# Other costs, handovers and priorities for the list that orders an attention stage

## The chip, the cores and the metric

The kernel runs on one core of a Trainium2 chip. The metric is the device time of one execution in microseconds, the median of several. The core has TensorE (PE, with weight loads shown apart as PEld), VectorE (DVE), ScalarE (ACT) and GpSimd (POOL), each with a queue that it works through in order, and SyncE (SP), which only issues transfers here. Five queues run side by side and wait for one another by semaphores; what stands where in each queue is fixed when the program is built.

## The reference

Two parts follow each other: a recurrent attention and an MLP.

```python
# r, k, v, w, a, b: (4, 8, 768, 40); w in 0.85 to 0.95
for t in range(S):
    y[:, :, t] = np.einsum('bhd,bhde->bhe', rt, state)
    Sa = np.einsum('bhde,bhe->bhd', state, at)
    state_decay = state * wt[:, :, None, :] - np.einsum('bhd,bhe->bhde', Sa, bt)
    state = state_decay + np.einsum('bhd,bhe->bhde', vt, kt)
...
x = y.transpose(0, 2, 1, 3).reshape(3072, 320)
h = x @ w_in                                   # 320 x 2048
sp = np.where(h > 20.0, h, np.log1p(np.exp(np.minimum(h, 20.0))))
out = (h * np.tanh(sp)) @ w_out                # 2048 x 320
```

Each of the 32 pairs of batch and head has a 40x40 state that every one of the 768 time steps decays and updates.

## The kernel before

The 768 steps are cut into 12 chunks of 64. Within a chunk the recurrence becomes matrix products with a triangular matrix that has to be inverted; between chunks only the state passes. There are four kinds of work:

- **Preparation** (`pre_a`, lines 241 to 332), once for each chunk and each `be` of 2, so 24 times. SP loads wa (decay and a) and bk (b and k). DVE forms running products of the decay with two scans (L266, L271), scales a and bk by them (L269, L277) and takes reciprocals; ACT lays a out (L275); PE forms the products of a and bk (L306), which ACT and DVE move from PSUM into GP and HA (L309 to L317), and transposes bk into bkn (L329, L331). POOL stores the running decay (L280). There is one wa buffer and one bk buffer for each `be`; the next load waits for the last reader, for bk that is L329.
- **Inverse** (`inv`, lines 334 to 396), once for a pair of chunks, so 6 times. DVE transposes GP into X (L338), then runs 30 rounds of a product (L343) and a sum (L346), each needing the one before, then transposes X to TT (L348) and TT back (L350). Small 32x32 products on PE (L361, L369) complete the blocks, ACT assembles them in bdT (L383 to L385), and PE and ACT make the KT tiles of both chunks (L393, L396).
- **Step** (`step`, lines 401 to 534), once for a chunk, 12 in a row, each half g of the heads by itself: copy of the state (L419), product with KT (L429, L432), products with bdr (L469, L472), transposes (L442, L457), output and state products (L497, L502) and the state update on DVE (L482, L507, L513). POOL loads VS, UVT and bdr (L403, L407, L410) and stores the output y (L533).
- **Weight conversions** for the MLP (`Mlp.plan`, lines 631 to 653): float64 weights are loaded by SP as integer pairs, turned into float32 by bit operations on DVE (L645 to L649) and split into a high and a low part (L651, L652). A first block of them becomes possible when all preparations are done, a second when all inverses are done.

Buffers bound how far one kind may run ahead: two GP tiles (one a pair), eight HA and eight bkn tiles (four chunks), four KT tiles (two chunks), one X and one TT, four PSUM banks for preparation and inverse and four for the steps.

The order of all this is not written by hand. `Plan.op` collects the operations with an engine, a cost, a latency `lat` until others may use the result, and the tiles read and written, from which it derives who must come after whom. Claims on pool buffers (`Buf`) are not among these links. `Plan.order` then plays the list through: `tail` of an operation is the longest sum of costs and latencies from it to the end; the engine that can start something first is picked, and of its operations that can start within `look` = 0.05 us of the earliest, the one with the longest tail is taken. An operation that needs a pool buffer can't start before one is free. PE pays 0.13 for a change of tile mode. The result, sorted by start, is emitted, so that it fixes every queue. `late=LATE`, 15.0, stands on one operation only, the state update L513, once per chunk and half; through the chain of states it adds 15 to the tail for every chunk still to come.

The MLP (`Mlp.run`, lines 718 to 793) follows outside this list, in plain program order; its first matmul is L751.

Of the kernel before, what the change touches and what calls it, by code (L numbers as in the profile page):

```python
# [7 lines left out]
F32 = mybir.dt.float32  # L8
# [10 lines left out]
LATE = 15.0  # L19
# [10 lines left out]

class Plan:


    def __init__(self, look=0.05):
        self.ops, self.wr, self.rd, self.free, self.look = [], {}, {}, {}, look
# [7 lines left out]
    def op(self, eng, cost, fn, r=(), w=(), lat=0.15, mode=None, late=0.0, claim=()):  # L43
        o = Op()
        o.eng, o.cost, o.fn, o.lat, o.mode, o.late, o.i = eng, cost, fn, lat, mode, late, len(self.ops)
# [25 lines left out]
    def after(self, ops, fn):  # L71
        key = ('after', len(self.ops))
        o = self.op('0', 0.0, fn, w=[key], lat=0.0)
        for p in ops:
            if p.i not in o.pre:
                o.pre[p.i] = p
                p.post.append(o)
        return key

    def order(self):  # L80
        for o in reversed(self.ops):
            o.tail = o.cost + o.lat + max((p.tail for p in o.post), default=0.0) + o.late
            o.need = len(o.pre)
            o.ready = 0.0
        ready = [o for o in self.ops if not o.need]
        clock, mode, out = {}, {}, []
        while ready:
            best = None
            start = {}
            for o in ready:  # L90
                t = max(o.ready, clock.get(o.eng, 0.0))
                for b in o.bufs:
                    if b.t is None:
                        free = self.free[b.pool[0]]
                        t = max(t, min((f for f in free if f is not None), default=1e9))
                start[o] = t
# [4 lines left out]
            best = max((o for o in ready if o.eng == e and start[o] <= low[e] + self.look), key=lambda o: (o.tail, -o.i))  # L101
# [8 lines left out]
            c = best.cost  # L110
            if best.mode and mode.get(e) not in (None, best.mode):
                c += 0.13
            mode[e] = best.mode or mode.get(e)
            end = t + c
            clock[e] = end
            best.start = t
            out.append(best)
            ready.remove(best)
            for b in best.bufs:
                b.users -= 1  # L120
                b.end = max(b.end, end + best.lat)
# [52 lines left out]
def attention(ctx, tc, I, yD, pD, nch, M):  # L174
# [66 lines left out]
    def pre_a(c, be):  # L241
        wa, bk, ad = wab[be], bkb[be], adb[be]
        xo, og, ok, oa, oh = (0, 0, 64, 0, 40) if be == 0 else (0, 64, 0, 64, 0)
        for al in range(2):
            q = slice(al * 64, al * 64 + 40)
            op('S', 0.1, lambda q=q, al=al: SP.dma_start(out=wa[q], in_=I['wa'][c, be, al]), w=[('wz', be, al), ('a', be, al)], lat=2.5)
        for al in range(2):
            q = slice(al * 64, al * 64 + 40)
            op('S', 0.1, lambda q=q, al=al: SP.dma_start(out=bk[q, :, xo:xo + 128], in_=I['bk'][c, be, al]), w=[('bk', be, al)], lat=2.5)
        if (c, be) == (0, 0):  # L250
            op('S', 0.1, lambda: SP.dma_start(out=cst, in_=I['cst']), w=['cst'], lat=2.5)
# [12 lines left out]
        op('V', 0.35, lambda: V.tensor_reduce(out=w2.t[:, 0], in_=wz3[:, :, 1:33], axis=AX.X, op=ALU.mult), r=WZ, w=[w2])  # L264
        op('V', 0.14, lambda: V.reciprocal(d1[:, 64:584:65], w2.t[:, 0]), r=[w2], w=['d1'])
        op('V', 1.15, lambda: V.tensor_tensor_scan(out=P.t, data0=wz[:, 0:520], data1=d1[:, 64:584], initial=0.0, op0=ALU.mult,  # L266
                                                   op1=ALU.add), r=WZ + ['d1'], w=[P])
        op('V', 0.1, lambda: V.tensor_copy(w2.t[:, 1], P.t[:, 64:520:65]), r=[P], w=[w2])
        op('V', 0.62, lambda: V.tensor_tensor(out=a3, in0=a3, in1=p3()[:, :, 0:64], op=ALU.mult), r=[P], w=AA)  # L269
        op('V', 0.14, lambda: V.reciprocal(d1[:, 64:584:65], w2.t[:, 1]), r=[w2], w=['d1'])  # L270
        op('V', 1.15, lambda: V.tensor_tensor_scan(out=E[:, 0:519][:, ::-1], data0=wz[:, 2:521][:, ::-1], data1=d1[:, 1:520][:, ::-1],  # L271
                                                   initial=0.0, op0=ALU.mult, op1=ALU.add), r=WZ + ['d1'], w=['E'])
        for al in range(2):
            q = slice(al * 64, al * 64 + 64)
            op('A', 0.58, lambda q=q, al=al: A.copy(ad[q, :, :, al], a[q].rearrange("p (s k t) -> p s k t", k=2, t=32)),  # L275
               r=[('a', be, al)], w=[('ad', be, al)])
        op('V', 1.14, lambda: V.tensor_tensor(out=bk4, in0=bk4, in1=E3[:, :, 0:64].unsqueeze(2).broadcast_to([128, 8, 2, 64]),  # L277
                                              op=ALU.mult), r=['E'], w=BK)
        for al in range(2):
            op('G', 0.6, lambda al=al: G.dma_start(out=pD[c, be, :, al], in_=P.t[al * 64:al * 64 + 40]), r=[P], lat=1.5)  # L280
        if be == 1:
# [9 lines left out]
            op('P', 0.3, mm, r=ws + ['cst'], w=[b], mode=64, claim=[rw])  # L291
# [7 lines left out]
        for s0 in (0, 3, 6):  # L299
# [8 lines left out]
            op('P', 0.29 * m, mm, r=[('ad', be, 0), ('ad', be, 1), ('id', be)] + BK, w=[b], mode=128, claim=[gp, ha])  # L308
            op('A', 0.2, lambda s0=s0, m=m, pv=pv: A.mul(gp.t[0:64, u0 + s0:u0 + s0 + m, 1], pv()[0:64, 0:m, og:og + 32], -1.0),  # L309
               r=[b], w=[(gp, u0 + s0)])  # L310
            op('A', 0.27, lambda s0=s0, m=m, pv=pv: A.mul(gp.t[64:128, u0 + s0:u0 + s0 + m].rearrange("p u k i -> p u (k i)"),
                                                          pv()[64:128, 0:m, og:og + 64], -1.0), r=[b], w=[(gp, u0 + s0, 1)])
            op('A', 0.21, lambda s0=s0, m=m, pv=pv: A.copy(ha.t[:, s0:s0 + m, oa:oa + 40], pv()[:, 0:m, 128:168]), r=[b], w=[(ha, s0)])  # L313
            op('V', 0.27, lambda s0=s0, m=m, pv=pv: V.tensor_tensor(out=ha.t[:, s0:s0 + m, oh:oh + 64], in0=pv()[:, 0:m, ok:ok + 64],
                                                                    in1=maskH.unsqueeze(1).broadcast_to([128, m, 64]), op=ALU.mult),
               r=[b, 'cst'], w=[(ha, s0 + 1)])
        op('V', 0.36, lambda: V.tensor_tensor(out=gp.t[:, u0:u0 + 8, 1], in0=gp.t[:, u0:u0 + 8, 1],  # L317
# [5 lines left out]
        for s0 in (0, 4):  # L323
# [6 lines left out]
            op('P', 0.45, tr, r=BK + ['cst'], w=[b], mode=128, claim=[bkn])  # L330
            op('A', 0.38, lambda s0=s0, pv=pv: A.copy(bkn.t[:, s0 * 80:s0 * 80 + 320].rearrange("p (s a e) -> p s a e", a=2, e=40),  # L331
                                                     pv()[:, :, :, 0:40]), r=[b], w=[(bkn, s0)])

    def inv(n):
# [3 lines left out]
        op('V', 2.0, lambda: V.transpose(X.rearrange("p t j -> p j t"), gp.t[:, :, 1].rearrange("p u j -> p j u")), r=allg, w=['X'])  # L338
        op('V', 0.08, lambda: V.memset(X.rearrange("p t j -> p (t j)")[:, 0:1024:33], 1.0), w=['X'])
        for i in range(1, 31):  # L340
            m = 31 - i
            tv = tmp[:, 0:m * i].rearrange("p (t j) -> p t j", j=i)
            op('V', 0.16 + m * i * 0.001, lambda tv=tv, i=i, m=m: V.tensor_tensor(  # L343
                out=tv, in0=X[:, i + 1:32, i:i + 1].broadcast_to([128, m, i]), in1=X[:, i:i + 1, 0:i].broadcast_to([128, m, i]), op=ALU.mult),
               r=['X'], w=['tmp'], lat=0.0)
            op('V', 0.16 + m * i * 0.001, lambda tv=tv, i=i: V.tensor_tensor(out=X[:, i + 1:32, 0:i], in0=X[:, i + 1:32, 0:i], in1=tv, op=ALU.add),  # L346
               r=['tmp'], w=['X'], lat=0.0)
        op('V', 1.9, lambda: V.transpose(TT.rearrange("p u t -> p t u"), X), r=['X'], w=['TT'])  # L348
        T1 = lambda: gp.t[0:64, :, 0]
        op('V', 1.15, lambda: V.transpose(T1(), TT[0:64]), r=['TT'], w=[(gp, 'T1')])  # L350
        for h in range(2):
# [18 lines left out]
            op('P', 0.85, mx, r=['TT'] + gk(h), w=[bx], mode=32)  # L370
            op('A', 0.54, lambda xv=xv: A.copy(X2, xv()), r=[bx], w=['X2'])
            op('P', 0.85, my, r=[(gp, 'T1'), 'X2'], w=[by], mode=32)
            c = 2 * n + h
            
            for be in range(2):
# [4 lines left out]
                for al in range(2):  # L380
                    q0 = slice(al * 32, al * 32 + 32)
                    q1 = slice(64 + al * 32, 96 + al * 32)
                    op('A', 0.37, lambda bd=bd, q0=q0, us=us, al=al: A.copy(bd[q0, :, al, 0:32], TT[q0, us]), r=['TT'], w=[bdk[al * 3]])  # L383
                    op('A', 0.37, lambda bd=bd, q1=q1, us=us, al=al: A.copy(bd[q1, :, al, 32:64], TT[q1, us]), r=['TT'], w=[bdk[al * 3 + 1]])
                    op('A', 0.34, lambda bd=bd, q0=q0, al=al, yv=yv, be=be: A.copy(bd[q0, :, al, 32:64], yv()[q0, be * 8:be * 8 + 8]), r=[by],  # L385
                       w=[bdk[al * 3 + 2]])
                for s0 in (0, 4):
# [7 lines left out]
                    op('P', 0.9, mk, r=[(ha, k) for k in (0, 1, 3, 4, 6, 7)] + bdk, w=[b], mode=128, claim=[kt])  # L395
                    op('A', 0.54, lambda s0=s0, kv=kv, kt=kt: A.copy(kt.t[:, s0:s0 + 4], kv()), r=[b], w=[(kt, s0 // 4)])  # L396
# [18 lines left out]
    def step_a(c, g):  # L415
        st = ST[g]
        if c > 0:
            for be in range(2):
                op('A', 0.42, lambda be=be: A.copy(VS[be][srow[be], g, 0:320].rearrange("p (s d) -> p s d", d=40), st[srow[be], :, 0:40]),  # L419
# [11 lines left out]
        op('P', 1.0, mm, r=[(k, g) for k in kts] + [(x, be, g) for x in ('VSv', 'VSs') for be in range(2)], w=[b], mode=64)  # L431
        op('A', 0.56, lambda: A.mul(UVT.rearrange("p s (x t) -> p x s t", t=64)[:, 0:4:3, g * 4:g * 4 + 4], uv(), -1.0), r=[b], w=[('u', g)])  # L432

    def step_u(c, g):
        if c < nch - 1:
            for be in range(2):
# [6 lines left out]
                op('P', 0.45, tr, r=UV(g) + ['cst'], w=[b], mode=128)  # L443
                op('A', 0.38, lambda be=be, tv=tv: A.copy(UVQ[be][:, g * 8:g * 8 + 8, 64:104], tv()[:, :, :, 0:40].rearrange("p s a d -> p (s a) d")),
# [381 lines left out]
```

## Time and profile before

| | us |
|---|---|
| median of 3 runs | 893.96 (891.82 to 895.59) |
| the profiled execution's own time | 897.87 |
| its span, first to last instruction | 895.7 |
| first matmul of the MLP in it | 536.66 |
| PE busy / DVE busy / ACT busy | 733.2 / 477.8 / 425.5 |
| mean granted TensorE clock | 0.886 |

The profile shows one execution. Its page gives the busy time of each engine, the span in 40 equal slices with the busy share of each in tenths and the granted clock of TensorE (PEclk), the DMA queues, and the chain of work that ended last. Beside it there are views with the busy time by stretches of the span, with every instruction of one engine in order of time (start, duration, engine, line, operation, what it writes and reads, and in brackets the idle time before it with what ended it), and with the sums of all waits. A line number is that of the kernel before.

### The profile page before, as it was taken

Reading aid. Unit: us, or ns where it says so; the run is one execution under the profiler, and the core shown is the slowest. Engines: PE = TensorE matmul, PEld = TensorE weight load, DVE = VectorE, ACT = ScalarE, POOL = GpSimd, SP = SyncE. Lnnn points to the kernel's source line nnn. Section 1 sums busy time; section 2 is a strip of 40 time slices with the busy share of each in tenths; the row PEclk is TensorE's granted clock in tenths of the full one; section 3 lists DMA queues with packets and bytes.
Section 4 is the critical chain, followed back from the end, with each engine's and each line's share of the span. In section 5 each row is a group of like instructions: output and inputs, shape, how many; then the busy total and the mean of one; then the engine's idle time right before and its main releaser. Section 6 shows DMA issues by size and latency. Waiting matters only on the chain.

```text
span 895.7 us, 18823 instructions
## 1 busy us (share of the span) xinstructions
PE 733.2 (82%) x7816; PEld 705.3 (79%) x7816; DVE 477.8 (53%) x975; ACT 425.5 (48%) x937; POOL 101.5 (11%) x166
## 2 busy tenths in 40 slices
PE   2625885969597677959795939999999999999998
PEld 2515784968586676849684939999999999999998
DVE  5798488658946974895386579422222221222110
ACT  4423853665476455636554847433333333333331
POOL 7100211211220211112111200000000000000000
PEclk9655987789698969888896979999999999999999
DMA  7321522242223313222222376311111111110000
GB/s 166 95 52 31 129 67 69 77 105 68 68 65 92 90 37 86 74 75 59 61 78 78 108 244 166 84 36 52 33 33 37 51 33 34 36 33 16 15 1 30
DMA packets 58212, 61.91 MB, mean 69 GB/s; under 512 B 25536, under 2 KB 48704, under 8 KB 58128
## 3 DMA queue, kind: packets, MB, share of 16 engines
q1 hardware_dynamic: 49296, 40.94, 16.3%
q0 software_dynamic: 8832, 19.79, 8.8%
q8 instruction: 61, 1.00, 0.5%
q14 instruction: 23, 0.19, 0.1%
HBM read 48.79 MB, written 11.86 MB: 68 GB/s over the span
## 4 chain that ended last, share of the span: by engine, by line
PE 66%; DVE 17%; DMA 6%; ACT 6%; issue 3%; POOL 1%; SPq 1%; DVEq 0%; ACTq 0%; POOLq 0%
PE ph L751 21%; PE pr L306 7%; PE po L772 6%; PE po L773 6%; PE po L771 6%; DVE XL L346 5%; DVE tmp L343 5%; DMA bk<-in_bk 4%; PE pl L469 3%; PE pr L393 3%; PE pl L497 3%; PE pl L442 3%; PE pr L361 2%; PE pr L369 2%; DMA wa<-in_wa 2%
## 5 line engine op out<-in xcount | busy, mean ns | idle before, releaser
L751 PE MATMUL ph<-xh,w_ih 128*128 128x256 f32 x576 | 149.5, 285 | 14.7 <-ACT xh L734 14.7
L753 ACT ACTIVATE g<-ph 128x512 f32<-128x512 f32 x96 | 57.0, 597 | 187.8 <-PE ph L751 187.8
L757 DVE TENSOR_TENSOR gl<-g,gh 128x1024 fp32r<-128x1024 f32 x48 | 58.8, 1225 | 163.2 <-ACT gh L756 162.9
L306 PE MATMUL pr<-bk,ad 128*128 128x168 f32 x384 | 97.3, 418 | 52.9 <-ACT HA L313 17.8
L306 PEld LDWEIGHTS pr<-bk,ad 128*128 128x128 f32 x384 | 82.2, 266 | 60.5 <-ACT HA L313 20.2
L751 PE MATMUL ph<-xh,w_il 128*128 128x256 f32 x576 | 124.1, 284 | 0.0
L751 PEld LDWEIGHTS ph<-xh,w_ih 128*128 128x128 f32 x576 | 110.5, 192 | 15.1 <-ACT xh L734 15.0
L772 PE MATMUL po<-w_ol,gh 128*128 128x320 f32 x384 | 118.6, 309 | 0.0
L773 PE MATMUL po<-w_oh,gl 128*128 128x320 f32 x384 | 118.5, 309 | 0.0
L771 PE MATMUL po<-w_oh,gh 128*128 128x320 f32 x384 | 118.4, 308 | 0.0
L751 PE MATMUL ph<-xl,w_ih 128*128 128x256 f32 x384 | 101.3, 285 | 0.0
L751 PEld LDWEIGHTS ph<-xh,w_il 128*128 128x128 f32 x576 | 96.9, 192 | 0.0
L751 PEld LDWEIGHTS ph<-xl,w_ih 128*128 128x128 f32 x384 | 73.8, 192 | 0.1
L361 PE MATMUL pr<-TT,GP 32*32 32x32 f32 x768 | 21.7, 236 | 61.7 <-DVE TT L348 53.2
L771 PEld LDWEIGHTS po<-w_oh,gh 128*128 128x128 f32 x384 | 72.2, 188 | 0.0
L773 PEld LDWEIGHTS po<-w_oh,gl 128*128 128x128 f32 x384 | 72.1, 188 | 0.0
L772 PEld LDWEIGHTS po<-w_ol,gh 128*128 128x128 f32 x384 | 72.1, 188 | 0.0
L361 PEld LDWEIGHTS pr<-TT,GP 32*32 32x32 f32 x768 | 21.0, 151 | 63.0 <-DVE TT L348 34.8
L346 DVE TENSOR_TENSOR XL<-XL,tmp 128x30 f32<-128x30 f32 (+9 forms) x180 | 59.6, 331 | 5.6
L343 DVE TENSOR_TENSOR tmp<-XL 128x30 f32<-128x30 f32 (+9 forms) x180 | 59.6, 331 | 5.5
L393 PE MATMUL pr<-bdT,HA 128*104 128x128 f32 x384 | 54.8, 309 | 2.7 <-ACT HA L313 1.0
L393 PEld LDWEIGHTS pr<-bdT,HA 128*104 128x104 f32 x384 | 52.8, 201 | 4.6 <-ACT KT L396 1.6
(95 smaller groups left out, 1246.3 us busy)
## 6 DMA issues: line engine op xcount, KB each, us to landing
wa<-in_wa SPq DMA_DIRECT2D x48, 162.5 KB
bk<-in_bk SPq DMA_DIRECT2D x48, 160.0 KB
cv_d<-in_wi SPq DMA_DIRECT2D x12, 512.0 KB
cv_d<-in_wo SPq DMA_DIRECT2D x8, 640.0 KB
pD<-P POOLq DMA_DIRECT2D x48, 81.2 KB, 2.3
VS<-in_vN POOLq DMA_DIRECT2D x24, 160.0 KB, 3.0
bdr<-in_rD POOLq DMA_DIRECT2D x24, 160.0 KB, 4.5
UVT<-in_vD POOLq DMA_DIRECT2D x24, 160.0 KB, 3.7
```

What stands on the lines that cost most here:

```text
L306: PE.matmul(pv()[:, j], ad[:, s0 + j].rearrange("p k a t -> p (k a t)"), bk[:, s0 + j], start=(j == 0), stop=True, skip_group_check=True)
L343: op('V', 0.16 + m * i * 0.001, lambda tv=tv, i=i, m=m: V.tensor_tensor(out=tv, in0=X[:, i + 1:32, i:i + 1].broadcast_to([128, m, i]), in1 ...
L346: op('V', 0.16 + m * i * 0.001, lambda tv=tv, i=i: V.tensor_tensor(out=X[:, i + 1:32, 0:i], in0=X[:, i + 1:32, 0:i], in1=tv, op=ALU.add), ...
L361: PE.matmul(xv()[al * 32:al * 32 + 32, j], gp.t[q, u, 0], TT[q, u], start=(j == 0), stop=True, skip_group_check=True)
L393: PE.matmul(kv()[:, j], ha.t[:, s0 + j], bd[:, o + s0 + j].rearrange("p a t -> p (a t)"), start=(j == 0), stop=True, skip_group_check=True)
L442: PE.transpose(tv()[:, s].rearrange("p a d -> p (a d)"), UVT[:, g * 4 + s, be * 128:be * 128 + 128], ident)
L751: PE.matmul(o, w, x, start=(j == 0 and n == 0), stop=(n == 7), skip_group_check=True)
L753: A.activation(g[:, f0:f0 + 2], ph, AF.Mish)
L757: V.tensor_tensor(out=gl, in0=g, in1=gh.bitcast(F32), op=ALU.subtract)
L771: PE.matmul(po[k], gh[:, j, t], oh, start=(f == 0), stop=False, skip_group_check=True)
L772: PE.matmul(po[k], gh[:, j, t], ol, start=False, stop=False, skip_group_check=True)
L773: PE.matmul(po[k], gl[:, j, t], oh, start=False, stop=(f == 15), skip_group_check=True)
```

## The change

Only the arithmetic of the list and its numbers change; the operations, their tiles and the pool sizes stay. Every cost is replaced by a duration. An engine is taken to be free again after `occ`, 0.085 us before the end on DVE and 0.01 after it on ACT; a result is there after `fin`, which adds 0.16 on PE and, for transfers, a landing time; a dependent operation is ready `sem` later, 0.035 to 0.06 by its engine; a freed buffer costs 0.05. On PE the list keeps an account of busy time in windows of 4096/1200 = 3.41 us and from it a clock of 1.0 or 0.5; at 0.5 an operation takes `work` longer. LATE becomes 0.

```diff
-LATE = 15.0
+LOOK = 0.05
+LATE = 0.0
...
-    def op(self, eng, cost, fn, r=(), w=(), lat=0.15, mode=None, late=0.0, claim=()):
+    def op(self, eng, dur, fn, r=(), w=(), lat=None, mode=None, work=0.0, late=0.0, claim=(), tag=''):
...
+        o.occ = max(0.0, dur + dict(V=-0.085, A=0.01).get(eng, 0.0))
+        o.fin = dur + (lat if lat is not None else 0.16 if eng == 'P' else 0.0)
...
     def order(self):
+        sem = dict(V=0.035, A=0.035, P=0.053, S=0.06, G=0.06)
         for o in reversed(self.ops):
-            o.tail = o.cost + o.lat + max((p.tail for p in o.post), default=0.0) + o.late
+            o.tail = o.fin + 0.04 + max((p.tail for p in o.post), default=0.0) + o.late
...
+            occ, fin = best.occ, best.fin
+            if e == 'P':
+                if mode not in (None, best.mode):
+                    t += 0.095
+                mode = best.mode
+                while win < int(t / WINDOW):
+                    a = act.get(win, 0.0) / WINDOW
+                    clk = (1.0 if a >= 0.35 else 0.5) if clk == 1.0 else (1.0 if a >= 0.69 else 0.5)
+                    win += 1
+                if clk < 1.0:
+                    occ, fin = occ + best.work, fin + best.work + 0.04
...
+            clock[e] = t + occ
...
-                    self.free[b.pool[0]][b.k] = b.end
+                    self.free[b.pool[0]][b.k] = b.end + 0.05
...
-                p.ready = max(p.ready, end + best.lat)
+                p.ready = max(p.ready, t + fin + sem.get(p.eng, 0.0))
```

The numbers of the operations, some of about forty (the last number of a transfer is its landing):

```diff
-            op('S', 0.1, lambda q=q, al=al: SP.dma_start(out=wa[q], ...), ..., lat=2.5)
+            op('S', 0.45, lambda q=q, al=al: SP.dma_start(out=wa[q], ...), ..., lat=3.6)
-            op('S', 0.1, lambda q=q, al=al: SP.dma_start(out=bk[q, :, xo:xo + 128], ...), ..., lat=2.5)
+            op('S', 0.85, lambda q=q, al=al: SP.dma_start(out=bk[q, :, xo:xo + 128], ...), ..., lat=3.7)
-        op('V', 1.15, lambda: V.tensor_tensor_scan(out=P.t, ...
+        op('V', 1.235, lambda: V.tensor_tensor_scan(out=P.t, ...
-        op('V', 1.14, lambda: V.tensor_tensor(out=bk4, ...
+        op('V', 1.22, lambda: V.tensor_tensor(out=bk4, ...
-            op('P', 0.29 * m, mm, ..., mode=128, claim=[gp, ha])
+            op('P', 0.286 * m, mm, ..., mode=128, work=0.28 * m, claim=[gp, ha])
-            op('V', 0.16 + m * i * 0.001, ..., r=['X'], w=['tmp'], lat=0.0)
+            op('V', (0.16 + m * i * 0.00104), ..., r=['X'], w=['tmp'])
-            op('P', 0.85, mx, ..., mode=32)
+            op('P', 1.15, mx, ..., mode=32, work=0.12)
-                    op('P', 0.9, mk, ..., mode=128, claim=[kt])
+                    op('P', 0.89, mk, ..., mode=128, work=0.7, claim=[kt])
-        op('P', 1.0, mm, ..., mode=64)
+        op('P', 0.95, mm, ..., mode=64, work=0.7)
-            op('P', 0.92, mm, r=UV(g) + [('bdr', 0, g), ('bdr', 1, g)], w=[b], mode=128)
+            op('P', 0.89, mm, r=UV(g) + [('bdr', 0, g), ('bdr', 1, g)], w=[b], mode=128, work=0.85)
-            op('V', 0.62, lambda be=be, qv=qv: V.tensor_tensor(
+            op('V', 0.69, lambda be=be, qv=qv: V.tensor_tensor(
-            op('P', 1.2 if c else 0.75, mm, ..., mode=64)
+            op('P', 1.2 if c else 0.75, mm, ..., mode=64, work=1.1 if c else 0.7)
-            op('V', 0.42, lambda: V.tensor_tensor(out=st[:, :, 0:40], ..., late=LATE)
+            op('V', 0.49, lambda: V.tensor_tensor(out=st[:, :, 0:40], ..., late=LATE)
```

More of the change, by code (lines that the diff above doesn't have):

```diff
@@ L28, with __init__ @@
     pass
+WINDOW = 4096 / 1200
 class Plan:
-    def __init__(self, look=0.05):
+    def __init__(self, look=LOOK):
         self.ops, self.wr, self.rd, self.free, self.look = [], {}, {}, {}, look
@@ L41, in pool @@
         return lambda: Buf((name, tiles))
-    def op(self, eng, cost, fn, r=(), w=(), lat=0.15, mode=None, late=0.0, claim=()):
+    def op(self, eng, dur, fn, r=(), w=(), lat=None, mode=None, work=0.0, late=0.0, claim=(), tag=''):
         o = Op()
-        o.eng, o.cost, o.fn, o.lat, o.mode, o.late, o.i = eng, cost, fn, lat, mode, late, len(self.ops)
+        o.eng, o.fn, o.mode, o.work, o.late, o.i, o.tag = eng, fn, mode, work, late, len(self.ops), tag
+        o.occ = max(0.0, dur + dict(V=-0.085, A=0.01).get(eng, 0.0))
+        o.fin = dur + (lat if lat is not None else 0.16 if eng == 'P' else 0.0)
         o.pre, o.post, o.bufs = {}, [], []
@@ L72, in after @@
         key = ('after', len(self.ops))
-        o = self.op('0', 0.0, fn, w=[key], lat=0.0)
+        o = self.op('0', 0.0, fn, w=[key])
         for p in ops:
@@ L80, in order @@
     def order(self):
+        sem = dict(V=0.035, A=0.035, P=0.053, S=0.06, G=0.06)
         for o in reversed(self.ops):
-            o.tail = o.cost + o.lat + max((p.tail for p in o.post), default=0.0) + o.late
-            o.need = len(o.pre)
-            o.ready = 0.0
+            o.tail = o.fin + 0.04 + max((p.tail for p in o.post), default=0.0) + o.late
+        for o in self.ops:
+            o.prio = o.tail
+            o.need, o.ready = len(o.pre), 0.0
         ready = [o for o in self.ops if not o.need]
-        clock, mode, out = {}, {}, []
+        clock, out = {}, []
+        mode, clk, win, act = None, 0.5, 0, {}
         while ready:
-            best = None
             start = {}
@@ L93, in order @@
                     if b.t is None:
-                        free = self.free[b.pool[0]]
-                        t = max(t, min((f for f in free if f is not None), default=1e9))
+                        t = max(t, min((f for f in self.free[b.pool[0]] if f is not None), default=1e9))
                 start[o] = t
@@ L100, in order @@
             e = min(low, key=low.get)
-            best = max((o for o in ready if o.eng == e and start[o] <= low[e] + self.look), key=lambda o: (o.tail, -o.i))
+            best = max((o for o in ready if o.eng == e and start[o] <= low[e] + self.look), key=lambda o: (o.prio, -o.i))
             t = start[best]
@@ L109, in order @@
                     b.t, b.end = True, 0.0
[L110 to L116, printed above, removed]
+            occ, fin = best.occ, best.fin
[9 more added lines that the diff above has]
+                    occ, fin = occ + best.work, fin + best.work + 0.04
+                k, x = win, best.work / clk
+                act[k] = act.get(k, 0.0) + min(x, (k + 1) * WINDOW - t)
+                if t + x > (k + 1) * WINDOW:
+                    act[k + 1] = act.get(k + 1, 0.0) + t + x - (k + 1) * WINDOW
+            clock[e] = t + occ
+            best.start, best.stop = t, t + fin
             out.append(best)
@@ L410, in step_loads @@
             op('G', 0.85, lambda q=q, al=al: G.dma_start(out=bdr[q, :, :, al].rearrange("p b s t -> p (b s) t"), in_=I['rD'][c, al]),
-               w=[('bdr', al, 0), ('bdr', al, 1)], lat=2.5)
+               w=[('bdr', al, 0), ('bdr', al, 1)], lat=3.9)
     UV = lambda g: [('UVv', 0, g), ('UVv', 1, g), ('u', g)]
@@ L418, in step_a @@
             for be in range(2):
[L419 removed]
+                op('A', 0.45, lambda be=be: A.copy(VS[be][srow[be], g, 0:320].rearrange("p (s d) -> p s d", d=40), st[srow[be], :, 0:40]),
                    r=[('ST', g)], w=[('VSs', be, g)])
@@ L430, in mm @@
                                   kts[be].t[:, g * 4 + s, al * 64:al * 64 + 64], start=(be == 0 and s == 0), stop=True, skip_group_check=True)
-        op('P', 1.0, mm, r=[(k, g) for k in kts] + [(x, be, g) for x in ('VSv', 'VSs') for be in range(2)], w=[b], mode=64)
-        op('A', 0.56, lambda: A.mul(UVT.rearrange("p s (x t) -> p x s t", t=64)[:, 0:4:3, g * 4:g * 4 + 4], uv(), -1.0), r=[b], w=[('u', g)])
+        op('P', 0.95, mm, r=[(k, g) for k in kts] + [(x, be, g) for x in ('VSv', 'VSs') for be in range(2)], w=[b], mode=64, work=0.7)
+        op('A', 0.6, lambda: A.mul(UVT.rearrange("p s (x t) -> p x s t", t=64)[:, 0:4:3, g * 4:g * 4 + 4], uv(), -1.0), r=[b], w=[('u', g)])
     def step_u(c, g):
```

114 lines of the change are left out of this document (57 added, 57 removed).

## The prediction

> **What bounds the kernel now.** I read the page's head first, then busy time by stage, then DVE and PE in order of time through one period, then the chain that ended last. The head:
>
> ```profile
> span 895.7 us, 18823 instructions
> PE 733.2 (82%) x7816; PEld 705.3 (79%) x7816; DVE 477.8 (53%) x975; ACT 425.5 (48%) x937; POOL 101.5 (11%) x166
> PE   2625885969597677959795939999999999999998
> DVE  5798488658946974895386579422222221222110
> PEclk9655987789698969888896979999999999999999
> ```
>
> One slice is 22.4 us. From slice 24 on PE stands at 9: that is the MLP, which the list doesn't order. Before it PE and DVE take turns. The stages, cut at the transposes that end an inverse (L348):
>
> ```profile
> core 0: us, PE busy (x) PEld busy (x) DVE busy (x) ACT busy (x) POOL busy (x), PEclk, DMA share, GB/s
> 70.50:152.65 82.15, 61.26 (x832) 57.36 (x832) 60.29 (x143) 46.82 (x122) 15.08 (x24) 0.81 0.30 80
> 235.18:316.24 81.06, 61.48 (x864) 56.63 (x864) 57.67 (x137) 45.64 (x120) 15.09 (x24) 0.86 0.28 75
> 316.24:398.14 81.90, 61.81 (x864) 57.15 (x864) 57.64 (x137) 45.72 (x120) 15.11 (x24) 0.85 0.28 74
> 518.50:536.60 18.10, 3.44 (x91) 3.20 (x86) 13.28 (x21) 7.79 (x14) 1.00 (x2) 0.66 0.73 222
> 536.60:895.70 359.10, 355.67 (x2688) 355.17 (x2688) 100.70 (x113) 135.19 (x196) 0.00 (x0) 0.99 0.16 44
> 70.50:479.35 408.85, 310.46 (x4280) 288.48 (x4280) 289.45 (x681) 229.96 (x602) 73.44 (x116) 0.84 0.28 75
> ```
>
> Five periods take 408.85 us, 81.8 each. In a quiet one PE is busy 61.5 us and DVE 57.7: neither fills it. Finer cuts show the turns:
>
> ```profile
> 160.00:180.00 20.00, 19.72 (x291) 18.93 (x292) 11.27 (x24) 13.58 (x33) 4.77 (x8) 0.85 0.30 83
> 180.00:200.00 20.00, 12.52 (x110) 11.51 (x108) 11.26 (x26) 12.44 (x37) 3.80 (x6) 0.83 0.42 109
> 200.00:220.00 20.00, 18.01 (x226) 16.73 (x220) 18.61 (x48) 11.63 (x30) 2.27 (x4) 0.91 0.17 45
> 220.00:240.00 20.00, 10.43 (x231) 9.46 (x230) 17.54 (x44) 8.14 (x20) 4.27 (x6) 0.77 0.35 82
> ```
>
> The fuller of the two engines adds up to 19.72 + 12.52 + 18.61 + 17.54 = 68.4 of 80, a share of 0.855. What a better order can win is the turn-taking itself. DVE in order of time shows why they take turns:
>
> ```profile
> 152.65 1.91 DVE L348 STREAM_TRANSPOSE TT<-XL 128x1024 f32<-128x1024 f32 x1
> 154.42 1.20 DVE L277 TENSOR_TENSOR bk<-bk,E 128x1024 f32<-128x1024 f32 x1
> 190.52 1.23 DVE L277 TENSOR_TENSOR bk<-bk,E 128x1024 f32<-128x1024 f32 x1 [5.39 <-DMA bk<-in_bk]
> 198.56 1.23 DVE L277 TENSOR_TENSOR bk<-bk,E 128x1024 f32<-128x1024 f32 x1 [1.44 <-DMA bk<-in_bk]
> 205.39 2.14 DVE L338 STREAM_TRANSPOSE XL<-GP 128x1024 f32<-128x1024 f32 x1
> 214.02 0.38 DVE L343 TENSOR_TENSOR tmp<-XL 128x210 f32<-128x210 f32 x1
> 214.43 0.38 DVE L346 TENSOR_TENSOR XL<-XL,tmp 128x210 f32<-128x210 f32 x1
> 217.31 2.48 DVE L472 TENSOR_TENSOR UVQ<-pl,cst 128x512 f32<-128x512 f32 x4
> 219.70 0.40 DVE L343 TENSOR_TENSOR tmp<-XL 128x238 f32<-128x238 f32 x1
> 235.18 1.91 DVE L348 STREAM_TRANSPOSE TT<-XL 128x1024 f32<-128x1024 f32 x1
> 236.95 1.19 DVE L277 TENSOR_TENSOR bk<-bk,E 128x1024 f32<-128x1024 f32 x1
> ```
>
> The next pair's preparation (L277 among it) starts right behind a TT transpose, at 154.42, and runs to 205; then the inverse has DVE from 205.39 to 237. No preparation instruction for the pair after it runs in that stretch, only the chunk's own L472, L507 and L513. Its next bk product stands at 236.95, behind TT. PE, in order of time, pays for it:
>
> ```profile
> 216.95 1.91 PE L329 MATMUL pr<-cst,bk 128*128 128x128 f32 x16
> 237.14 3.09 PE L361 MATMUL pr<-TT,GP 32*32 32x32 f32 x108 [8.14 <-DVE TT L348]
> ```
>
> L329 is the last reader of the bk buffer. Its input came from the L277 at 198.56 and was ready at 199.8, yet it ran at 216.95, so the next bk load went late too. Then PE stood 8.14 us.
>
> **The change part by part.** No instruction is added or removed; only the order on each queue can differ, PE, DVE, ACT, and the transfers on SP and POOL.
>
> *Inverse links.* Before, a link hands over to the next with no delay (lat 0.0), so at every pick it ties with whatever is ready and wins by its tail. After, DVE counts as free 0.085 us before an instruction's end, and the dependent link as ready 0.035 after it. The 0.12 between exceeds the look-ahead of 0.05, so a pick always falls on another ready DVE instruction, whatever its tail. The trace bears both numbers out: the link at 214.43 follows one of 0.38 us by 0.41 (+0.03), while four independent L472 of about 0.69 take 2.48 us, 0.09 of overlap at each joint. About 60 joints an inverse turn from +0.035 to -0.085: 7 us of DVE, so DVE needs 51 to 58 us a period.
>
> *Who fills the joints.* Per pair, DVE has 12 x 4 = 48 preparation instructions and 6 x 4 = 24 step instructions, 72 against 62 of the inverse. Nearly all can lie between links, and the 51 us in which the preparation now stands alone (154.42 to 205.39) and the inverse's 30 merge. The buffers allow it: two GP tiles, and HA and BKN for four chunks.
>
> *The slope.* With LATE = 15 a step's tail rises by the listed 6.4 us of its state chain (0.45 + 0.95 + 0.6 + 0.89 + 0.69 + 1.2 + 0.315 + 0.49, three times 0.16 behind PE, eight times 0.04) plus 15: 21 a chunk, 43 a pair. An inverse adds 27 (19.9 for the 60 links, 60 x 0.04, two transposes 4.2, the memset 0.2). So before, a step goes before the next inverse. Without it a step's tail rises 13 a pair. Preparation and inverse rank first on every engine, L329 with them (its tail holds the next bk load). Steps fall behind, until the four KT and eight BKN buffers make the others wait. On POOL, VS, UVT and bdr loads move with the steps and may come to stand in front of pD stores; POOL is busy 15 of 82 us, so I cost this at nothing. If that cover goes, a step's slowest load shows, at most once per chunk:
>
> ```profile
> bdr<-in_rD POOLq DMA_DIRECT2D x24, 160.0 KB, 4.5
> ```
>
> *SP.* Listed issue goes from 0.1 to 0.45 and 0.85, landing from 2.5 to about 3.7: two bk loads come to 2 x 0.85 + 3.7 = 5.4. They share SP's queue with the wa loads and the conversions' loads, and come earlier there as L329 does. The chain in order of time measured more:
>
> ```profile
> 183.89 6.53 DMA bk<-in_bk
> 266.16 6.49 DMA bk<-in_bk
> ```
>
> So the new list is still 1.1 us short on a bk load. The L277 behind it stands in DVE's queue with the inverse links behind it, and PE's L361 behind those. Bounds: nothing, or 4 x 1.1 = 4.4 us a period; I take 3, since most loads have no slack in a packed list.
>
> *PE.* Its work a period is 61.5 us at a mean clock of 0.84 over the five periods. Bounds: all of it again, or 61.5 x 0.84 = 52 at full clock. I take 57, since fewer gaps raise the clock, but the 32x32 groups (L361) stay thin.
>
> The row first on the clock:
>
> ```profile
> 60.00:80.00 20.00, 5.60 (x134) 5.14 (x134) 18.16 (x42) 4.51 (x12) 1.02 (x2) 0.50 0.07 19
> ```
>
> PE busy 5.6 of 20 us ran at 0.50. [...]
>
> *Sum of a period.* 57 / 0.855 = 67, and 3 for late loads: 70. Five periods are 350 instead of 408.85: -59. Keeping 0.855 is my choice; it is what this program reaches in a period with the turns. The start and the end balance: the first inverse is stretched by the second pair's preparation, and the last period has none to carry.
>
> *The end.* From the chain in order of time:
>
> ```profile
> 495.24 2.02 PE pl L429 x64
> 507.55 3.67 PE pr L393 x32
> 521.51 0.46 PE pl L502 x8
> 529.36 4.35 DMA cv_d<-in_wo
> 536.66 3.37 PE ph L751 x13
> ```
>
> One chunk's step takes 495.24 to 507.55 = 12.3 us when nothing else stands beside it. Without the slope I expect one more chunk left over after the last inverse: +12.3 (bounds 0 and 24.6). The weight conversions, which today keep the MLP from 522 to 536.66, then lie partly beside that step: -4 (bounds 0 and -14.7). Net +8.
>
> Sum: -59 + 8 = -51. The profiled execution took 897.87 us (span 895.7), 3.9 over the median of 893.96. 897.87 - 51 = 847 on its scale, **843** on the median's.
>
> **The rivals.**
>
> *PE at full clock throughout.* If the filled inverse stretches leave no slow window, a period is 52 / 0.855 + 3 = 64; -89 + 8 = -81: 813. For it: 0.91 in 200 to 220 us. Against: 0.85 at 160 to 180 with PE full, since it starts slow. [...]
>
> *Stalls in order.* An inverse link now stands behind other instructions, and each of them that comes late delays the whole inverse. The gain of 12 us a period is gone when 72 such instructions are late by 0.17 us on average. At 0.1 us, 7 us goes: period 77, -24 + 8 = -16: 878. For it: the waits of DVE,
>
> ```profile
> DVE bk L277 <- DMA bk<-in_bk: 31.9, 9, 5.6
> DVE UVQ L472 <- PE pl L469: 22.2, 18, 8.3
> ```
>
> of which today only L472, L507 and L513 can stop an inverse. Against: the new durations are nearer to the rows (L277 listed at 1.14, now 1.22). The row at 190.52 shows DVE idle for 5.39 us with L264 and L271 listed behind. [...]
>
> *The steps are left behind* (the other side). Last everywhere, steps hold KT and BKN, so the preparation two pairs ahead waits for them: L329 for the bkn tile, the bk load for L329. The overlap then hardly comes (period 80, -9), and three more chunks remain after the last inverse, where DVE has little to do: +37. Total +28: 922. It decides from the point where chunks left over x 12.3 exceed 5 x (81.8 - period). For it: nothing in the tails stands for a buffer. Against: in the forecast the chain from TT over the KT products (8 us by the listed costs, 1.15 + 0.58 + 1.15 + 1.2 + 3.6 + 0.6), a step (12.3), L329 (0.9), a load (6.5), L277 (1.2) and L306 (2.3) is 31 us, well below 70.
>
> *The order hardly changes:* few instructions are ready in the joints, since loads and PSUM set them: period 82, 894.
>
> **How the numbers follow.** Forecast 0.48 (period 66 to 74: 823 to 863); full clock 0.14; stalls 0.16; steps left behind 0.15; no change 0.07. The range 800 to 900 leaves out the far end of the full clock (0.06) and most of the steps left behind (0.13). Of this kernel a measurement can tell about 0.5%, 4.5 us, from no change. Faster: 0.48 + 0.14 + 0.14 = 0.76; within 0.5%: 0.08; slower: 0.16.
>
> **What would show it.** Right: TT transposes about 70 us apart; L343 and L346 alternating with L266, L271, L277 and L269; L277 no longer right behind TT; the idle time before L361 well under 8 us; PEclk in the periods near 0.9. For the end: step work (L469, L497) after the last TT for more than two chunks, and a shorter gap to L751. Wrong: inverse and preparation still in separate stretches (no change); idle DVE before L277, L314 or L472 amid links (stalls); L429 to L502 of three or more chunks behind the last inverse and periods of 80 (steps left behind).

## The result, and the profile after

The changed kernel takes 800.41 us (median, 798.8 to 801.8) against 894.19 us for the kernel before in the same runs: a ratio of 0.8953 with a 95% interval of 0.8927 to 0.8979. The forecast was 843 with a range of 800 to 900. The direction came as forecast, and so did the merging of inverse and preparation; the gain was 94 us where 51 were forecast. That the time lies inside the range by only 0.4 us is luck: kernels with nearly the same list, further down, took 787 to 825 us.

The page of the changed kernel, its first lines: span, busy time, and 40 slices of 20 us each. The lines of the changed kernel stand 18 further down (L295 was L277, L366 was L348, L379 was L361, L769 was L751).

```profile
span 798.8 us, 18810 instructions
PE 698.0 (87%) x7816; PEld 676.8 (85%) x7816; DVE 457.9 (57%) x975; ACT 419.3 (52%) x937; POOL 101.4 (13%) x166
PE   3734599998999974999972999999999999999998
DVE  5899999989984699996446962122212222221110
PEclk9868598997999997999986899999999999999999
```

PE and DVE no longer take turns: from slice 6 to 12 both stand at 8 or 9. One pair of 7 and 4 on PE is left (slices 15 and 16), with DVE's own 4 and 6 just ahead (slices 13 and 14). The busy time by stages, again cut at the transposes to TT, has first the five periods one by one, then all five, then the end of the attention and the MLP:

```profile
core 0: us, PE busy (x) PEld busy (x) DVE busy (x) ACT busy (x) POOL busy (x), PEclk, DMA share, GB/s
87.65:128.51 40.86, 37.53 (x590) 35.87 (x589) 38.87 (x105) 32.12 (x84) 6.51 (x10) 0.85 0.27 69
128.51:186.33 57.82, 55.22 (x850) 52.35 (x846) 52.52 (x129) 43.37 (x119) 13.53 (x21) 0.94 0.35 96
186.33:240.44 54.11, 51.14 (x786) 48.74 (x788) 48.72 (x124) 40.22 (x109) 12.10 (x20) 0.91 0.41 102
240.44:333.02 92.58, 75.34 (x1092) 69.60 (x1088) 69.78 (x171) 58.66 (x161) 21.32 (x34) 0.94 0.34 87
333.02:365.00 31.98, 31.34 (x642) 29.49 (x641) 30.30 (x86) 24.79 (x61) 9.75 (x14) 1.00 0.29 74
87.65:365.00 277.35, 250.58 (x3945) 236.05 (x3944) 240.20 (x612) 199.15 (x531) 63.22 (x98) 0.93 0.34 88
422.00:439.95 17.95, 2.94 (x78) 2.69 (x73) 12.34 (x19) 8.52 (x15) 1.00 (x2) 0.65 0.71 218
439.95:798.80 358.85, 355.43 (x2688) 355.02 (x2688) 100.56 (x113) 134.53 (x194) 0.00 (x0) 0.99 0.16 44
```

Where the time went can be added up from these rows and those of before. The five periods went from 408.85 to 277.35: -131.5. The first TT comes at 87.65 instead of 70.50: +17.2. From the last TT to the MLP's first matmul it takes 365.00 to 439.95 = 75.0 instead of 479.35 to 536.66 = 57.3: +17.6. Together -96.7, and the span is 96.9 shorter. The MLP takes what it took (358.85 and 359.10).

DVE in order of time shows the filled joints, links of the inverse (L361, L364) and the preparation of the next pair (L295, L289) in turn:

```profile
227.88 1.22 DVE L295 TENSOR_TENSOR bk<-bk,E 128x1024 f32<-128x1024 f32 x1 [1.30 <-PE pl L487]
229.02 0.36 DVE L364 TENSOR_TENSOR XL<-XL,tmp 128x198 f32<-128x198 f32 x1
229.29 1.23 DVE L289 TENSOR_TENSOR_SCAN E<-wa,d 128x519 f32<-128x519 f32 x1
230.44 0.33 DVE L361 TENSOR_TENSOR tmp<-XL 128x184 f32<-128x184 f32 x1
230.68 1.22 DVE L295 TENSOR_TENSOR bk<-bk,E 128x1024 f32<-128x1024 f32 x1
```

Each starts 0.08 to 0.09 us before the one ahead of it ends, as the change lists it. And PE hardly waits for TT any more. The groups of the 32x32 products, the first of the kernel before (61.7 us idle ahead of them), the second of the changed kernel (2.9 us):

```profile
L361 PE MATMUL pr<-TT,GP 32*32 32x32 f32 x768 | 21.7, 236 | 61.7 <-DVE TT L348 53.2 <-DVE R L482 8.6
```

```profile
L379 PE MATMUL pr<-TT,GP 32*32 32x32 f32 x768 | 16.1, 202 | 2.9 <-DVE TT L366 2.3 <-issue 0.6
```

### The profile page after: what moved, and what is told of

Same layout as the page of the kernel before. It is cut to its first block, busy times and chain, and to the rows that moved or that the text cites. A ratio compares the mean times of both kernels' runs of the same rounds, so it can differ in the third digit from the quotient of the medians.

```text
span 798.8 us, 18810 instructions
## 1 busy us (share of the span) xinstructions
PE 698.0 (87%) x7816; PEld 676.8 (85%) x7816; DVE 457.9 (57%) x975; ACT 419.3 (52%) x937; POOL 101.4 (13%) x166
## 4 chain that ended last, share of the span: by engine, by line
PE 69%; DVE 13%; ACT 5%; DMA 5%; issue 5%; POOL 2%; SPq 0%; DVEq 0%; ACTq 0%; POOLq 0%
PE ph L769 23%; PE po L791 7%; PE po L790 7%; PE po L789 7%; PE pl L487 5%; PE pr L324 4%; PE pr L411 4%; PE pl L515 3%; PE pl L447 2%; PE pl L460 2%; DVE XL L364 2%; DVE tmp L361 2%; DVE bk L295 2%; DVE P L284 2%; DMA bk<-in_bk 2%
## 5 line engine op out<-in xcount | busy, mean ns | idle before, releaser
L769 PE MATMUL ph<-xh,w_ih 128*128 128x256 f32 x576 | 149.4, 285 | 15.0 <-ACT xh L752 15.0
L324 PE MATMUL pr<-bk,ad 128*128 128x168 f32 x384 | 77.9, 363 | 57.8 <-DVE HA L332 33.6
L769 PE MATMUL ph<-xh,w_il 128*128 128x256 f32 x576 | 124.0, 284 | 0.0
L769 PEld LDWEIGHTS ph<-xh,w_ih 128*128 128x128 f32 x576 | 110.4, 192 | 15.3 <-ACT xh L752 15.3
L324 PEld LDWEIGHTS pr<-bk,ad 128*128 128x128 f32 x384 | 69.5, 230 | 62.4 <-DVE HA L332 35.2
L769 PE MATMUL ph<-xl,w_ih 128*128 128x256 f32 x384 | 101.2, 285 | 0.0
L769 PEld LDWEIGHTS ph<-xh,w_il 128*128 128x128 f32 x576 | 96.9, 192 | 0.0
L769 PEld LDWEIGHTS ph<-xl,w_ih 128*128 128x128 f32 x384 | 73.7, 192 | 0.1
L364 DVE TENSOR_TENSOR XL<-XL,tmp 128x30 f32<-128x30 f32 (+9 forms) x180 | 58.8, 327 | 2.4
L361 DVE TENSOR_TENSOR tmp<-XL 128x30 f32<-128x30 f32 (+9 forms) x180 | 58.6, 326 | 2.5
L487 PE MATMUL pl<-bdr,UVT 128*128 128x128 f32 x384 | 50.9, 291 | 3.3 <-issue 2.8
L411 PE MATMUL pr<-bdT,HA 128*104 128x128 f32 x384 | 49.0, 285 | 3.5 <-ACT bdT L403 3.2
L487 PEld LDWEIGHTS pl<-bdr,UVT 128*128 128x128 f32 x384 | 48.3, 205 | 4.3 <-issue 3.1
L774 ACT CAST gh<-g 128x1024 fp32r<-128x1024 f32 x48 | 50.3, 1047 | 1.2
```

What stands on the lines that cost most here:

```text
L324: PE.matmul(pv()[:, j], ad[:, s0 + j].rearrange("p k a t -> p (k a t)"), bk[:, s0 + j], start=(j == 0), stop=True, skip_group_check=True)
L361: op('V', (0.16 + m * i * 0.00104), lambda tv=tv, i=i, m=m: V.tensor_tensor(out=tv, in0=X[:, i + 1:32, i:i + 1].broadcast_to([128, m, i]), ...
L364: op('V', (0.16 + m * i * 0.00104), lambda tv=tv, i=i: V.tensor_tensor(out=X[:, i + 1:32, 0:i], in0=X[:, i + 1:32, 0:i], in1=tv, op=ALU.ad ...
L411: PE.matmul(kv()[:, j], ha.t[:, s0 + j], bd[:, o + s0 + j].rearrange("p a t -> p (a t)"), start=(j == 0), stop=True, skip_group_check=True)
L487: PE.matmul(qv()[:, s], UVT[:, g * 4 + s, be * 128:be * 128 + 128], bdr[:, be, g * 4 + s].rearrange("p a t -> p (a t)"), start=(s == 0), s ...
L769: PE.matmul(o, w, x, start=(j == 0 and n == 0), stop=(n == 7), skip_group_check=True)
```

## The experiments

**Three parts, all eight combinations.** My theory was that the new handover on DVE (the links of the inverse no longer tied to each other) makes the gain. The rivals were that the missing slope makes it, or the new durations, load delays and clock account. Each of the three can be undone or done alone by an edit of a line or two.

The slope put back in the changed kernel (e1), and taken from the kernel before (e2):

```diff
-LATE = 0.0
+LATE = 15.0
```

> The changed kernel with the slope of 15 a chunk put back, all else as changed. If the handover on DVE makes the gain (links of the inverse no longer tied to one another), steps merely rank first again and the time stays between 800 and 825 us. If the missing slope makes it, most of the gain goes: 870 to 895. If the new durations and the clock account make it, 800 to 810.

> The kernel before with nothing changed but the slope, 15 to 0. Handover theory: links still win every pick on DVE and steps now rank last, so 880 to 910. Slope theory: 805 to 830. Durations theory: about 894.

The joints alone, in the kernel before (e3):

```diff
-               r=['X'], w=['tmp'], lat=0.0)
+               r=['X'], w=['tmp'], lat=0.12)
...
-               r=['tmp'], w=['X'], lat=0.0)
+               r=['tmp'], w=['X'], lat=0.12)
```

> The kernel before with its old costs and its slope, and one number changed: the latency of the inverse's links from 0.0 to 0.12 us, so that a link is no longer ready at the instant the one before ends. Handover theory: the preparation fills the joints and the time falls to 810 to 840. Slope theory and durations theory: 880 to 895.

The links tied again in the changed kernel (e4):

```diff
-               r=['X'], w=['tmp'])
+               r=['X'], w=['tmp'], lat=-0.12)
...
-               r=['tmp'], w=['X'])
+               r=['tmp'], w=['X'], lat=-0.12)
```

> The changed kernel with its durations and without slope, but with the links tied again (their result ready 0.12 us earlier, at the instant DVE counts as free). Handover theory: inverse and preparation part again, 860 to 890. Slope theory and durations theory: 800 to 815.

None of the three theories got its numbers in all four runs. Only e3 fell into a forecast, the 880 to 895 of the slope and durations theories; e1, e2 and e4 lie outside all of theirs. So the two combinations that were missing came next: e5 is e2 and e3 together, e9 is e1 and e4 together. Both fell between their two cases.

> The kernel before, old costs, with both single edits at once: links' latency 0.12 and slope 0. Alone they gave 7 and 18 us. If they only add, 868 to 872. If they need each other (joints are only worth filling when the preparation may go first, and it can only go first into joints), 815 to 845, and the durations make what is left to 800.

> The changed kernel with the links tied and the slope of 15 put back, so that only the durations, load delays, handovers of other operations and the clock account are new. If these are worth something by themselves, 855 to 875; if only the pair of joints and slope makes the gain, 885 to 895.

| durations | joints open | slope | kernel | us | ratio to before, interval |
|---|---|---|---|---|---|
| old | no | 15 | before | 893.6 | 1 |
| old | yes | 15 | e3 | 886.32 | 0.991 (0.9876 to 0.9943) |
| new | no | 15 | e9 | 878.37 | 0.9817 (0.9787 to 0.9847) |
| old | no | 0 | e2 | 875.36 | 0.978 (0.9734 to 0.9826) |
| old | yes | 0 | e5 | 854.74 | 0.9562 (0.9521 to 0.9602) |
| new | no | 0 | e4 | 849.93 | 0.9509 (0.9479 to 0.9538) |
| new | yes | 15 | e1 | 833.59 | 0.9324 (0.9303 to 0.9345) |
| new | yes | 0 | the change | 800.41 | 0.8953 (0.8927 to 0.8979) |

"New" durations stand for all the rest of the change: durations, load delays, handovers of the other operations and clock account. By themselves the joints are worth 7 us, the durations 15 and the slope 18, 41 in all; together they are worth 94. Opening the joints gains 7 and 21 with the old durations, 45 and 50 with the new. The new durations gain 15 and 25 with the joints shut, 53 and 54 with them open. So joints and durations look like a pair in which each needs the other. The slope's removal gains 18 to 33 in all four places. One side effect of the edits was not tried apart: `lat` is part of the tail, so e3 and e5 raise an inverse's tail by 60 x 0.12 = 7.2 us, and e4 and e9 lower it by as much.

That the joints are worth little with the old durations is not for lack of filling. Counted in DVE's order of time, 218 of the 354 joints between links hold something else in e3 and 213 in the changed kernel, against 33 in the kernel before; PE's wait for TT falls from 53.2 us to 2.1 in e3 too. Its five periods take 362.10 us instead of 408.85, but its first TT comes at 105.61 instead of 70.50, so that 12 us of the span are left, 7 in the median. The waits of DVE for the bk load show part of what is wrong, for e3, e5, e9 and the changed kernel in this order (total us, times, longest):

```profile
DVE bk L277 <- DMA bk<-in_bk: 36.4, 13, 5.0
```

```profile
DVE bk L277 <- DMA bk<-in_bk: 30.1, 12, 4.8
```

```profile
DVE bk L295 <- DMA bk<-in_bk: 14.0, 6, 4.0
```

```profile
DVE bk L295 <- DMA bk<-in_bk: 4.8, 4, 1.7
```

And DVE of e3 in order of time shows what such a wait does once the joints are open:

```profile
290.91 0.33 DVE L343 TENSOR_TENSOR tmp<-XL 128x168 f32<-128x168 f32 x1
295.94 1.23 DVE L277 TENSOR_TENSOR bk<-bk,E 128x1024 f32<-128x1024 f32 x1 [4.70 <-DMA bk<-in_bk]
297.09 0.33 DVE L346 TENSOR_TENSOR XL<-XL,tmp 128x168 f32<-128x168 f32 x1
```

The list placed L277 into a joint at a time when, by its old numbers (0.1 to issue, 2.5 to land), the load was there. It was not, and the link behind it, whose input was ready at 291.2, stood until 297.09. The short listing is only part of this wait: the load was not issued before 291.28, when L329 (289.28 to 291.25) had freed the buffer, and then took 4.66 us. This is the rival "stalls in order", measured.

The fairest pair is e3 and e1, which have the joints and the slope in common. The bk waits are 36.4 and 4.0 us in all, the times 53 us apart. It is clearest ahead of the first TT, where DVE has nearly the same work in both (busy 76.7 and 77.3 us): TT comes at 105.61 in e3 and at 88.80 in e1, and DVE's waits for bk and wa loads up to there are 20.4 and 6.3 us, 14 of the 17 us. So in that stretch late loads are most of the difference. What makes the rest, and how much each of the new numbers does, was not tried one by one.

What e4 shows is the other half: new durations, joints shut. Only 49 of its 354 joints hold something else. Two of its inverses, the second and the sixth, from X to TT, in busy time by stretch:

```profile
97.36:124.09 26.73, 16.78 (x268) 15.61 (x268) 24.64 (x66) 12.74 (x32) 1.25 (x2) 0.78 0.15 43
411.52:436.72 25.20, 8.62 (x104) 7.74 (x104) 23.14 (x64) 5.76 (x15) 1.48 (x2) 0.73 0.18 55
```

In the second, DVE does little but the inverse's own instructions (x66), and PE is busy 16.8 of 26.7 us at a clock of 0.78. The sixth has no next preparation that could stand beside it; PE is busy 8.6 of 25.2 us there, at 0.73. The next row of PE in order of time begins with the only wait of PE for TT in this kernel:

```profile
438.69 1.54 PE L379 MATMUL pr<-TT,GP 32*32 32x32 f32 x50 [18.29 <-DVE TT L366]
```

**The clock account.** In e6 the list takes TensorE's clock as full throughout (`clk = 1.0`); nothing else is edited.

> The changed kernel with a list that takes TensorE's clock as full throughout, all else as changed. If the clock account does nothing, since the filled stages run near full clock anyway, 798 to 805. If it places PE work well, 812 to 830.

It took 823.19 us (0.9207, 0.9183 to 0.9231), 23 us more than the change. By the expectation this speaks for the account; the next runs show why I don't take it as settled.

**The long fourth period.** Period four is 92.58 us long where its neighbours are 54 and 32. DVE in order of time has the reason:

```profile
268.64 0.75 DVE L282 TENSOR_REDUCE w<-wa 128x8 f32<-128x256 f32 x2 [5.23 <-PE pr L307]
```

L282 starts the preparation of chunk 8. It writes a w2 tile, of which there are four, and L307 frees one by reading it. L307 came at 268.20, behind step work on PE; my reading is that it ranks low because no tail holds a pool buffer. PE was full while DVE had little to do:

```profile
240.00:260.00 20.00, 19.58 (x374) 18.20 (x372) 8.18 (x16) 14.57 (x36) 5.49 (x8) 1.00 0.41 87
260.00:280.00 20.00, 19.58 (x307) 18.44 (x305) 13.21 (x25) 15.96 (x40) 6.18 (x11) 1.00 0.39 100
```

In e7 there are eight:

```diff
-    newW2 = make(cp, 4, [128, 2, 8], "w2")
+    newW2 = make(cp, 8, [128, 2, 8], "w2")
```

> The changed kernel with eight w2 tiles instead of four. In its trace DVE stands idle from 245 to 268 us but for step work, until L307 frees a w2 tile, and the fourth period is 93 us long. If that wait costs what it looks like, the fourth period falls by 15 to 20 and the time to 783 to 792. If PE, full from 240 to 280, is the bound there, the steps only move and it is 796 to 803.

It took 812.17 us (0.909, 0.9064 to 0.9115): slower by 12, and both cases of the expectation missed. The transposes to TT of e7 tell what became of the gain:

```profile
186.11 1.97 DVE L366 STREAM_TRANSPOSE TT<-XL 128x1024 f32<-128x1024 f32 x1
261.62 1.98 DVE L366 STREAM_TRANSPOSE TT<-XL 128x1024 f32<-128x1024 f32 x1
327.39 1.99 DVE L366 STREAM_TRANSPOSE TT<-XL 128x1024 f32<-128x1024 f32 x1
```

The fourth period did fall, from 92.58 to 65.77, but the third rose from 54.11 to 75.51, and the five together from 277.35 to 283.89. DVE's waits for bk loads, 4.8 us in the change, came to 21.2, 7.4 of them in the third period; what else lengthened it stays open:

```profile
DVE bk L295 <- DMA bk<-in_bk: 21.2, 9, 7.2
```

**How much is the list's own scatter?** A buffer more that makes a kernel slower suggested that any edit shuffles the picks. Four runs looked at that: the look-ahead at 0.04 (e10), a slope of 4 (e8), the landing of bk at 4.8 (e11), and a slope of 3 with a look-ahead of 0.03 (e12).

```diff
-LOOK = 0.05
+LOOK = 0.04
```

> The changed kernel with the look-ahead at 0.04 us instead of 0.05. Both lie well under the 0.12 between one link and the next, so no rule of the list changes and only single picks fall otherwise. If a list of this kind has a settled time, 797 to 804. If it jumps with small edits, as the 12 us that eight w2 tiles cost suggest, it is off by 5 to 20 us to either side.

```diff
-LATE = 0.0
+LATE = 4.0
```

> The changed kernel with a slope of 4 a chunk. A step's tail then rises by about 21 a pair, still under the 27 of an inverse, so the preparation still ranks first. If the loss of 33 us at a slope of 15 comes from the rank of steps above the next inverse, this stays within 800 to 810. If it grows with the slope, about 809. If the list jumps, anything between 800 and 835.

```diff
-            op('S', 0.85, lambda ...: SP.dma_start(out=bk[q, :, xo:xo + 128], ...), w=[('bk', be, al)], lat=3.7)
+            op('S', 0.85, lambda ...: SP.dma_start(out=bk[q, :, xo:xo + 128], ...), w=[('bk', be, al)], lat=4.8)
```

> The changed kernel with the landing of the bk loads listed at 4.8 instead of 3.7 us, which makes two of them the 6.5 us of the traces. If late loads cost the changed kernel the 3 us a period of the forecast, 785 to 795. If DVE's waits for bk (4.8 us in all in its trace) are all there is, 795 to 805, or later where the list jumps.

```diff
-LOOK = 0.05
-LATE = 0.0
+LOOK = 0.03
+LATE = 3.0
```

> The changed kernel with a slope of 3 and a look-ahead of 0.03: steps a little earlier, so that fewer are left over, without ranking above an inverse. If the long fourth period and the three chunks behind the last inverse are what is left to win, 785 to 795. If not, 800 to 820.

| kernel | us | against the change | ratio to before, interval |
|---|---|---|---|
| e10, look-ahead 0.04 | 789.74 | -10.7 | 0.8845 (0.882 to 0.8871) |
| e8, slope 4 | 824.62 | +24.2 | 0.9236 (0.921 to 0.9262) |
| e11, bk landing 4.8 | 817.47 | +17.1 | 0.9153 (0.9121 to 0.9185) |
| e12, slope 3, look-ahead 0.03 | 786.51 | -13.9 | 0.8799 (0.8767 to 0.8832) |

Edits that change no rule, or hardly one, move the time by -14 to +24 us, far outside the intervals; slopes of 3 and 4 lie 38 us apart. So differences of that size between two lists say little about the edit that separates them. That holds for the clock account (+23), and for e11, which landed above both cases of its forecast although its wait for bk stayed as small as that of the change:

```profile
DVE bk L295 <- DMA bk<-in_bk: 5.7, 1, 5.7
```

It also weakens each single slope result (18 to 33 us), though all four point the same way, and the 7, 15, 21 and 25 us of joints and durations alone. What stands well clear of it is the whole (94 us), the opening of the joints under the new durations (45 and 50), and the new durations with the joints open (53 and 54). Every list with one of the three parts undone (833.59 us and more) is also slower than the four of this table and than e6 and e7. That joints and durations need each other rests on 38 and 29 us more, each a difference of four lists, and is likely rather than shown. How far the old list scatters was not tried.

e10 and e12 beat both kernels. In e10 the gain lies behind the last TT (60.6 us to the MLP instead of 75.0) and not in the periods (279.70). In e12 it lies in the periods. From its first TT to the last, and from there to the MLP:

```profile
86.97:347.72 260.75, 239.25 (x3835) 224.04 (x3836) 239.62 (x606) 194.22 (x514) 61.46 (x96) 0.95 0.36 91
347.72:426.17 78.45, 57.13 (x1067) 54.36 (x1063) 45.02 (x79) 51.76 (x111) 15.22 (x23) 0.92 0.51 152
```

The five periods lose another 17 us, and PE and DVE are now both busy for 92% of them (239.25 and 239.62 of 260.75). The long fourth period is gone: it takes 56.11. Three chunks still stand behind the last inverse, and the end is 3.5 us longer than in the change.

## Why the prediction was right, and where its sizes were off

*Inverse links, and who fills the joints:* right, by the rows at 227.88 to 230.68 and by e4. The 0.12 us against a look-ahead of 0.05 is what opens the joints. That this does little by itself (e3, 7 us, with as many joints filled) I had not foreseen, and it takes weight from two of my signs, the alternating links and the short wait before L361: e3 shows both. (The stretch of the kernel before from 205.39 to 237, where I saw only L472, L507 and L513 beside the inverse, also has one L314 and one L652; that changes nothing.)

*SP:* I treated the new load delays as a small cost still open, 3 us a period for bk loads listed 1.1 us short. In the changed kernel these waits are 4.8 us in all, 1 a period, and listing them longer (e11) gained nothing. The step missed what the new numbers do once the joints are open: with the old ones, at the same slope, these waits are 36.4 us (e3), with the new 4.0 (e1).

*The sum of a period* is the step that was mis-sized: 57 / 0.855 + 3 = 70 on paper, 277.35 / 5 = 55.5 measured. Not all of that is gained. 335 of 4280 PE instructions (x4280 to x3945) left the periods for the time before the first TT and behind the last, and come back in the +17.2 and +17.6. Over the whole attention PE's busy time fell from 733.2 - 355.67 = 377.5 to 698.0 - 355.43 = 342.6, 35 us or 7 a period, while the clock in the periods rose from 0.84 to 0.93. Like for like, if all 35 us are put down to the periods, PE needs 62.1 - 7 = 55 us a period (62.1 is 310.46 / 5), near the 57 that I took. (The lower bound of 52 at full clock was an estimate, 61.5 x 0.84; the five periods of the changed kernel had 0.93.) The period from 333.02 to 365.00, with PE busy 31.34 of 31.98 us, ran at a clock of 1.00. The share of 0.855 was wrong in two ways. It was the share of the fuller of the two engines, stretch by stretch, and I divided PE's work alone by it, whose own share was 310.46 / 408.85 = 0.76. And it was a share reached with turns: taken in the same way, in stretches of 20 us, it rose to 0.96. PE's own came to 250.58 / 277.35 = 0.90. With 55 / 0.90 = 61, waits for loads included, a period is 9 us shorter than the 70: 45 us in five, and the span fell by 46 us more than the 51 forecast. The 9 come from three terms of like size: the share makes 55 / 0.855 - 61 = 3, the loads 3 and PE's need 2 / 0.855 = 2.3. Of the rivals, *PE at full clock throughout* (period 64, 813 us) was nearer than the forecast, and it too kept the 0.855. The turns themselves were the loss, so their share was a number not to carry over.

*The start and the end balance:* the first TT came 17.2 us later, and the last period was 32 us, 23 under the mean. Right in kind. But TT transposes "about 70 us apart", a sign that I named, did not come: they lie 32 to 93 us apart.

*The end:* one more chunk left over, as forecast. The step's first product of the last three chunks, from PE in order of time:

```profile
367.78 2.09 PE L447 MATMUL pl<-KT,VS 104*64 104x64 f32 x64
388.69 2.08 PE L447 MATMUL pl<-KT,VS 104*64 104x64 f32 x64
406.97 1.15 PE L447 MATMUL pl<-KT,VS 104*64 104x64 f32 x32 [1.15 <-ACT yev L527]
```

All three stand behind the last TT at 365.00, where it was two chunks before. But the -4 for the conversions did not come. They are no earlier beside the steps: from 422.00 to 439.95 PE is busy 2.94 of 17.95 us, as before from 518.50 to 536.60. The last chunk was also slower: from its L447 at 406.97 it took 7.57 us until L487 began, and L487 took 6.63, where the same two took 2.75 and 3.84 before. These are 7.6 us for which the forecast had no term. The granted clock was 0.55 during this L487 (414.54 to 421.17) and 1.00 during the one before (L469, 514.34 to 518.18); for the 2.85 us that PE stood idle just ahead of L487 the trace names no releaser. Forecast +8, measured +17.6.

*The slope, and the steps left behind:* in this rival the missing slope costs 28 us; its removal gained in all four places. Yet the rival's mechanism is there, on a smaller buffer than I named: not KT or bkn but w2 held the preparation in the fourth period. There, from 240 to 280 us, PE did step work and DVE idled. It cost less than the overlap gained. The rival's deciding point was chunks left over x 12.3 above 5 x (81.8 - period); it came to one chunk more against 5 x 26.3 us.

*The order hardly changes:* wrong, by every row above.

## What to carry to other kernels

When two engines take turns, estimate a reordering from the work of each engine and not from the share that they reach while taking turns. Filling the gaps of a chain on DVE gained little here (7 us in e3) while the list had the data of the inserted work land too early: in e3 a product whose load came late stood in front of the whole chain (4.70 us of idle DVE), and filled gaps alone were no sign of a gain. This greedy list jumped by -14 to +24 us of 800 with edits that mean next to nothing, so try several neighbours and compare rules over more than one pair of lists before crediting one.

## What the runs showed of the hardware

On DVE, an instruction that needed nothing from the one ahead started 0.08 to 0.09 us before that one ended (229.02 + 0.36 = 229.38, next start 229.29, in the changed kernel), and one that needed its result about 0.03 us after (214.02 + 0.38 = 214.40, next start 214.43, in the kernel before). Interleaving two chains saved that 0.12 us at a joint on DVE itself, beside the overlap with PE: over the whole attention the time in which DVE was busy fell from 477.8 - 100.70 = 377.1 to 457.9 - 100.56 = 357.3 us with the same 975 instructions in all. The instructions did not get shorter (added up one by one they take 511.0 us before and 511.6 after, over the whole kernel); they overlap more. The forecast had 7 us for each of six inverses; 3.3 came, and 180 joints more were filled than before (213 against 33), 30 an inverse where the forecast had about 60.
